# A spectrum scratch laid out by slice, loaded with repeated source rows and stored in halves

## The chip, the cores and the metric

The kernel runs on one core of a Trainium2 chip. The metric is the device time of one execution in microseconds (us). The core has five engines that run their own instruction streams and meet at semaphores: TensorE (PE in the profile, with its weight loads as PEld), VectorE (DVE), ScalarE (ACT), GpSimd (POOL) and SyncE (SP). Here SP only issues transfers; POOL issues some too. Sixteen DMA engines move the data of all transfers.

## The reference

Four layers run one after the other on a sequence of 2048 tokens with 512 channels: a long convolution, an attention over a few neighbours, and both again with the same weights.

```python
x = A_u
x = x + _A_ref(_layernorm(x, axis=-1), ...)   # convolution
x = x + _B_ref(_layernorm(x, axis=-1), ...)   # local attention
x = x + _A_ref(_layernorm(x, axis=-1), ...)
x = x + _B_ref(_layernorm(x, axis=-1), ...)
```

Only the convolution matters here. It builds one filter per channel and multiplies in the frequency domain:

```python
P = jnp.exp(logdA[:, :, None] * l[None, None, :])
K = jnp.einsum("dn,dnl,dn->dl", Cc, P, dB).real
Kf = rfft(pad(K));  Uf = rfft(pad(u))
y = irfft(Uf * Kf)[:, :L] + u * Dskip
```

`Kf`, the spectrum of the filters, depends on the weights alone. Both convolutions use the same one.

## The kernel before, in words

**Making the spectrum (0 to about 126 us).** `kgen` builds tables of powers on VectorE, TensorE and ScalarE for one quarter of 128 channels after the other (`c` from 0 to 3). For each quarter TensorE multiplies the tables (`psk`), ScalarE copies the result (`KT`), and a round trip through a scratch in HBM brings it into another order (`rows_scratch`, L587 and L590). TensorE then turns it into frequencies in four steps (`spectrum`, `i` from 0 to 3, L601 and L606). ScalarE or VectorE writes the result into a tile `ks` of 128 channels x 2 x 512 (L614 to L630). There are four buffers for `ks`. The function `store` (L608) sends each tile to the HBM scratch `kt_scratch` with two transfers. That makes 16 tiles and 32 transfers, all issued by SP.

**Using it (about 119 to 152 us, and again 275 to 306 us).** The convolution runs over 16 slices of 32 channels (`cg`). For each slice TensorE transposes the signal (`pt`), VectorE copies it (`zt`), TensorE does the second stage of the Fourier transform (`xp`), ScalarE copies it (`xc`), VectorE multiplies it with the spectrum (`pab`, L275, the step `p`), TensorE transforms back (`vp`, L291) and ScalarE copies (`VT`, L295). The spectrum of a slice is a tile `Kt` of 128 partitions x 2048 elements, in which each row of 2048 elements stands twice, in an even partition and the odd one after it. `load_k` (L226) loads it from `kt_scratch` with two transfers, one into the even partitions and one into the odd. There are five buffers for `Kt` in the first convolution and six in the second. A load is issued when the product of the slice that had the buffer is done.

**What sets the order.** The order on the compute engines is written out by hand in two strings of step names (`KGEN` and `CONV2`). Transfers stand in the queue of the engine that issues them, in the order that the scheduler puts them. Slices 0 and 1 of the first convolution are issued by POOL, the others by SP. For the first four slices `FIRST_LOADS` names an instruction after which the load may be issued; for slices 2 and 3 that is a store. SP's transfers take eight semaphores in turn, and each transfer waits until the one eight places before it has landed.

Of the kernel before, what the change touches and what calls it, by code (L numbers as in the profile page):

```python
# [15 lines left out]
BF = mybir.dt.bfloat16  # L16
# [4 lines left out]
D = 512  # L21
# [8 lines left out]
GE = 4  # L30
# [4 lines left out]
DCH = 128  # L35
# [72 lines left out]
def make_small_consts(nc, const):  # L108
    fc = _fft_consts()
    C = {}  # L110
    C["F1_h"] = nc.inline_tensor(_bf(fc["F1"]), name="c_F1")
    C["F1T_h"] = nc.inline_tensor(_bf(fc["F1T"]), name="c_F1T")
    C["G_h"] = nc.inline_tensor(_bf(_kernel_dft()), name="c_G")
    bones_np = np.zeros((128, 8), dtype=np.float32)
    for f in range(128):
        bones_np[f, f // 16] = 1.0
    m, b, l, p = (x.ravel() for x in np.meshgrid(np.arange(2), np.arange(2), np.arange(16), np.arange(2), indexing="ij"))
    order = np.zeros((128, 128), dtype=np.float32)
    order[p * 64 + b * 32 + m * 16 + l, np.arange(128)] = 1.0
    small = [("order", _bf(order), BF), ("ident", _bf(np.eye(128)), BF), ("nident", _bf(-np.eye(128)), BF), ("nident4", _bf(-np.eye(128) * DH ** 0.5), BF),  # L120
             ("bones", _bf(bones_np), BF), ("C2", _bf(fc["C2"]), BF), ("IC", _bf(fc["IC"]), BF)]
    for name, arr, dt in small:
        h = nc.inline_tensor(arr, name="c_" + name)
        t = const.tile(list(arr.shape), dt, name="sb_" + name)
        C[name], C[name + "_h"] = t, h
    C["halves_h"] = nc.inline_tensor(_bf(_half_matrices()), name="c_halves")
    C["zero_h"] = nc.inline_tensor(_bf(np.zeros((1, 14 * 256))), name="c_zero")
    C["half_pi"] = const.tile([128, 1], F32, name="half_pi")
    nc.gpsimd.memset(C["half_pi"][:], np.pi / 2)
    C["zero"] = const.tile([128, 1], BF, name="zero_col")  # L130
    nc.gpsimd.memset(C["zero"][:], 0.0)
    C["den_bias"] = const.tile([128, 1], F32, name="den_bias")
    nc.gpsimd.memset(C["den_bias"][:], np.log(DEN_SCALE))
    C["eps"] = const.tile([128, 1], F32, name="eps")
    nc.gpsimd.memset(C["eps"][:], EPS)
    return C


def load_x(nc, const, x2d):
    xv = x2d.rearrange("(p j) d -> p j d", j=NJ)  # L140
    Xg = []
    for g in range(NG):
        t = const.tile([128, 4, D], BF, name=f"X{g}")
        nc.sync.dma_start(t[:], xv[:, g * 4:(g + 1) * 4, :])
        Xg.append(t)
    return Xg
# [24 lines left out]
def first_norm_tiles(small):  # L171
    return {n: small.tile([128, NJ] + e, F32, name="n1_" + n, bufs=1)
            for n, e in (("stats", [6]), ("mv", [2]), ("m2", []), ("den", []), ("rstd", []), ("nb", []))}
# [14 lines left out]
def first_norm_rstd(nc, st, eps, h):  # L188
    c = slice(h * NJ // 2, (h + 1) * NJ // 2)
    nc.scalar.activation(st["den"][:, c], st["m2"][:, c], ACT.Ln, scale=1.0 / D, bias=eps[:])  # L190
    nc.scalar.activation(st["rstd"][:, c], st["den"][:, c], ACT.Exp, scale=-0.5)
# [15 lines left out]
def z_view(Z):  # L207
    return Z[:].rearrange("k (c g) (r j e) -> k r j c g e", c=16, r=2, j=NJ)


def a_steps(nc, tc, C, Ng, kt_dram, load_w, layer, Z, es, es_y, psS=None):
# [4 lines left out]
    a = SimpleNamespace(es_y=es_y)  # L216
# [3 lines left out]
    kts, pts, zts, xps, xcs, pabs, vps = {}, {}, {}, {}, {}, {}, {}  # L220
# [4 lines left out]

    def load_k(cg, eng=nc.sync):  # L226
        kts[cg] = fwork.tile([128, 8, 2, 128], BF, name="Kt", tag="Kt", bufs=KT_BUFS[layer])
        rows = kt_dram.ap()[:, cg * 32:(cg + 1) * 32].rearrange("k (e g) a l -> k e (g a l)", e=GE)
        for h in range(2):
            eng.dma_start(kts[cg][h::2].rearrange("q g a l -> q (g a l)"), rows)  # L230

    def load_f1t():
        nc.sync.dma_start(F1T[:], C["F1T_h"].ap())
# [150 lines left out]
def kgen(nc, tc, C, prm, kt_dram, Zf, norm_row, norm_rstd, norm_apply, norm_apply_row, norm_tiles, load_rest, es_a, es_y, open_conv):  # L384
    everything = KGEN.split()
    with ExitStack() as es:
# [220 lines left out]

        def store(c, i, ks):  # L608
            for k in range(2):
                dst = kt_dram.ap()[k * 8 + i * 2:k * 8 + i * 2 + 2, c * DCH:(c + 1) * DCH]  # L610
                C["stored", c, i] = nc.sync.dma_start(dst.rearrange("k d r l -> d k (r l)"), ks[:, k, :].rearrange("d (k x) -> d k x", k=2))

        def spectrum_odd(c, i):
            ks = tiles["ks", c, i] = keep.tile([128, 2, 512], BF, name="ks", tag="ks", bufs=4)  # L614
# [72 lines left out]
        for c in range(4):  # L687
# [16 lines left out]
            for full in [n for n in everything if n.endswith(f":{c}") and n[0] in "Uv"]:  # L704
# [4 lines left out]
                else:  # L709
                    m = int(key[1:])  # L710
# [42 lines left out]
        for g in range(16):  # L753
# [7 lines left out]
            stored = [f"{'o' if g // 4 * 4 + i in WHOLE else 'e'}{g // 4}{i}" for i in range(4)]  # L761
# [852 lines left out]
@with_exitstack  # L1614
def kernel(
    ctx: ExitStack,
    tc: tile.TileContext,
    A_u: bass.AP,
    A_A_re: bass.AP,
    A_A_im: bass.AP,  # L1620
    A_B_re: bass.AP,
    A_B_im: bass.AP,
    A_C_re: bass.AP,
    A_C_im: bass.AP,
    A_log_dt: bass.AP,
    A_Dskip: bass.AP,
    B_x: bass.AP,
    B_wqkv: bass.AP,
    B_wo: bass.AP,
    out: bass.AP,  # L1630
):
    nc = tc.nc
    const = ctx.enter_context(tc.tile_pool(name="const", bufs=1))
    C = make_small_consts(nc, const)
    kt_dram = nc.dram_tensor("kt_scratch", (16, D, 2, 128), BF)
    C["rows_dram"] = nc.dram_tensor("rows_scratch", (4, 2, 2, 4, NV, 160), BF)
    prm = dict(A_re=A_A_re, A_im=A_A_im, B_re=A_B_re, B_im=A_B_im, C_re=A_C_re, C_im=A_C_im, log_dt=A_log_dt)
    C["out"] = out[0].rearrange("(p j) d -> p j d", j=NJ)
    Xg = []
    Ng = C["Ng"] = []  # L1640
    late = ctx.enter_context(tc.tile_pool(name="late", bufs=1, side="right"))
    C["small"] = ctx.enter_context(tc.tile_pool(name="small", bufs=2, side="right"))
    C["F1"] = late.tile([128, NJ, 2, 128], BF, name="F1sb")
    C["klast"] = late.tile([1, D], BF, name="klast")
    C["signs"] = late.tile([128, 2], BF, name="signs")
    for i in range(2):
        nc.gpsimd.memset(C["signs"][:, i:i + 1], 1.0 - 2 * i)
    C["last_tok"] = late.tile([128, 128], BF, name="last_tok")
    nc.gpsimd.memset(C["last_tok"][:], 0.0)
    nc.gpsimd.memset(C["last_tok"][0:1, 127:128], 1.0)  # L1650
    C["Drow"] = late.tile([128, D], BF, name="Drow")
    nc.gpsimd.memset(C["Drow"][:], 0.0)
    C["first_row"] = late.tile([128, 2 * NV], BF, name="first_row")
    nc.gpsimd.memset(C["first_row"][:], 0.0)
    nc.gpsimd.memset(C["first_row"][0:1, 2 * NV - 2:2 * NV], 1.0)
    n1 = {}

    def load_rest():
        for name in ("ident", "nident", "nident4", "bones", "C2", "IC"):
            nc.gpsimd.dma_start(C[name][:], C[name + "_h"].ap())  # L1660
        nc.gpsimd.dma_start(C["Drow"][0:1, :], A_Dskip.rearrange("(o d) -> o d", o=1))
        Xg.extend(load_x(nc, late, A_u[0]))
        nc.sync.dma_start(C["F1"][:], C["F1_h"].ap())
        n1["st"] = first_norm_tiles(C["small"])

    def norm_row(j, on_act):
        first_norm_row(nc, C["small"], n1["st"], Xg, j, on_act)

    def norm_rstd(h):
        first_norm_rstd(nc, n1["st"], C["eps"], h)  # L1670

    def norm_apply(h):
        first_norm_apply(nc, n1["st"], Xg, Ng, h)

    def norm_apply_row(j, on_act):
        first_norm_apply_row(nc, n1["st"], Xg, Ng, j, on_act)

    def norm_tiles():
        npool = ctx.enter_context(tc.tile_pool(name="normed", bufs=1, side="right", reuse_waits="tile"))
        Ng.extend(npool.tile([128, 4, D], BF, name=f"N{g}") for g in range(NG))  # L1680

    es_z = ExitStack()
    Z = es_z.enter_context(tc.tile_pool(name="a_z", bufs=1, reuse_waits="tile")).tile([128, NGR, 128], BF, name="Z")
    C["z_view"] = z_view(Z)
    es_y = ExitStack()
    Wt = {}

    def open_conv(psS):
        const2 = ctx.enter_context(tc.tile_pool(name="const2", bufs=1, side="right", reuse_waits="tile"))
        weights, load_w = load_b_weights(nc, const2, C, B_wqkv, B_wo)  # L1690
        Wt.update(weights)
        return a_steps(nc, tc, C, Ng, kt_dram, load_w, 0, Z, es_z, es_y, psS)

    a = kgen(nc, tc, C, prm, kt_dram, Z[:].rearrange("k a b -> k (a b)"), norm_row, norm_rstd, norm_apply, norm_apply_row, norm_tiles, load_rest, es_z, es_y, open_conv)
    es_z.close()
    for layer in range(2):
        y_rows, es_y = a_layer(nc, tc, C, Xg, Ng, kt_dram, layer, Z, es_z, a if layer == 0 else None)
        Z, es_z = b_layer(nc, tc, C, Xg, Ng, Wt, layer == 1, y_rows, es_y)
# [30 lines left out]
```

## Time and profile before

The median of three runs is 423.59 us (423.0 to 424.81). The profile is of one more execution.

| | before |
|---|---|
| median of the runs | 423.59 us |
| span of the profiled execution | 421.2 us |
| busy: PE, PEld, DVE, ACT, POOL | 90%, 61%, 94%, 79%, 6% |
| granted TensorE clock | 0.998 |
| DMA bytes, packets | 44.09 MB, 25822 |
| stores of the spectrum | 32 of 128 KB, issued 72.2 to 125.2 us |
| loads of the spectrum | 64 of 256 KB (60 from SP, 4 from POOL) |

The span runs from the first to the last instruction that the profiler recorded. The profile gives no time around it, so the difference of 2.4 us between span and median is taken as what lies outside the span and between executions. All times in views count from the start of the span. The DMA share is the mean busy share of the 16 DMA engines, so four full engines alone would show as 0.25. Times of packets can overlap a little, which is why a share can be a few per cent over 1.

### The profile page before, as it was taken

To read this page: it belongs to the slowest core of one execution; us is meant where nothing else is said; L and a number is where in the kernel's file an instruction comes from. 1 tells how busy PE (TensorE), PEld (TensorE's weight loads), DVE (VectorE), ACT (ScalarE), POOL (GpSimd) and SP (SyncE) were. 2 spreads that over 40 slices of the span, in tenths; PEclk is the share of its full clock that TensorE was granted. 3 is DMA by queue.
4 is the path that set the end of the run, shared out by engine and by line. 5 is a ranking of instruction groups with operands and counts; after the bars stand their busy time and mean duration, and the time that the engine had idled before them with its cause. 6 is when DMAs were issued, how large, how long until landed. Compare 5 with 4: busy or idle time off the path is not lost.

```text
span 421.2 us, 12212 instructions
## 1 busy us (share of the span) xinstructions
PE 377.2 (90%) x5088; PEld 259.0 (61%) x5131; DVE 396.4 (94%) x725; ACT 333.1 (79%) x601; POOL 26.0 (6%) x68
## 2 busy tenths in 40 slices
PE   1167998999989999999999999889999999998996
PEld 1033685676458755587866675278855686775663
DVE  6999999999889979899999999999989999999994
ACT  6999999998979979766665699989989576555452
POOL 5000011011210000002020000000000001200000
PEclk9999999999999999999999999999999999999999
DMA  7910001253899960005480029239500008160022
GB/s 219 424 53 0 3 14 50 76 163 101 256 246 273 259 208 4 2 2 95 83 174 6 2 70 232 103 103 262 139 0 4 2 2 174 37 142 4 2 102 101
DMA packets 25822, 44.09 MB, mean 105 GB/s; under 512 B 7317, under 2 KB 17238, under 8 KB 25126
## 3 DMA queue, kind: packets, MB, share of 16 engines
q1 hardware_dynamic: 22630, 37.30, 31.8%
q0 software_dynamic: 1888, 4.56, 5.0%
q10 hardware_dynamic: 1248, 1.44, 1.0%
q8 instruction: 40, 0.66, 0.7%
q14 instruction: 16, 0.13, 0.1%
HBM read 29.04 MB, written 6.95 MB: 85 GB/s over the span
## 4 chain that ended last, share of the span: by engine, by line
PE 48%; DVE 21%; DMA 8%; ACT 7%; issue 3%; SPq 1%; DVEq 0%; ACTq 0%
PE ps_qk L1207 8%; DVE prodpv L1403 6%; PE ps_o L1443 5%; PE ps_v L1294 5%; DMA V<-V 4%; PE po L1413 4%; DVE prodqk L1257 3%; PE psg L601 3%; PE vp L291 3%; PE Lp L1279 3%; DMA Kt<-kt_scratch 3%; DVE Z L504 2%; PE psk L568 2%; DVE pab L275 2%; ACT Z L1496 2%
## 5 line engine op out<-in xcount | busy, mean ns | idle before, releaser
L1403 DVE TENSOR_TENSOR prodpv<-V,Lsb 128x2048 bf16<-128x2048 bf16 x64 | 75.3, 1219 | 0.6 <-PE ps_max L1342 0.5
L1207 PE MATMUL ps_qk<-xnT,wqk 128*128 128x512 bf16 x256 | 60.0, 379 | 0.0
L1255 DVE TENSOR_TENSOR prodqk<-qT,N 128x1024 bf16<-128x1024 bf16 (+3 forms) x88 | 42.7, 541 | 2.0 <-ACT N L1210 1.8
L1257 DVE TENSOR_TENSOR prodqk<-qT,N 128x1024 bf16<-128x1024 bf16 (+3 forms) x56 | 39.9, 764 | 0.4 <-ACT N L1210 0.3
L275 DVE TENSOR_TENSOR pab<-xc,Kt 128x2048 bf16<-128x2048 bf16 (+1 forms) x34 | 38.8, 1154 | 1.2 <-DMA Kt<-kt_scratch 1.0
L1207 PEld LDWEIGHTS <-wqk 128*128 128x128 bf16 x256 | 23.5, 98 | 23.3
L1413 PEld LDWEIGHTS <-prodpv 128*128 128x128 bf16 x1024 | 33.6, 98 | 6.5 <-DVE prodpv L1403 2.1
L1413 PE MATMUL po<-halves,prodpv 128*128 128x64 bf16 x1024 | 36.5, 193 | 0.8 <-DVE prodpv L1403 0.6
L269 ACT CAST xc<-xp 128x1024 bf16<-128x1024 f32 (+1 forms) x34 | 34.6, 1033 | 2.2 <-PE xp L263 1.2
L291 PE MATMUL vp<-sb_IC,pab 128*128 128x128 bf16 x512 | 33.7, 219 | 1.6 <-DVE pab L275 0.7
L291 PEld LDWEIGHTS <-pab 128*128 128x128 bf16 x512 | 30.3, 98 | 7.4 <-DVE pab L275 4.0
L295 ACT CAST VT<-vp 128x1024 bf16<-128x1024 f32 (+1 forms) x31 | 32.6, 1067 | 1.1 <-PE vp L291 1.1
L1279 PEld LDWEIGHTS <-prodqk 128*128 128x128 bf16 x1024 | 30.1, 96 | 5.0 <-DVE prodqk L1257 1.4
L1443 PE MATMUL ps_o<-wo_t,oT 128*128 128x512 bf16 x124 | 32.3, 379 | 0.4
L1279 PE MATMUL Lp<-sb_bones,prodqk 128*128 128x8 bf16 x1024 | 30.9, 166 | 0.3
L1294 PE MATMUL ps_v<-wv,xnT 128*128 128x256 bf16 x256 | 30.6, 272 | 0.0
L528 PE MATMUL psadd<-Z,sb_ident 128*128 128x512 bf16 (+3 forms) x72 | 18.2, 334 | 13.1 <-DVE Z L504 7.7
L1160 DVE BATCH_NORM_STATS2 ln_stats<-X 128x6 f32<-128x512 bf16 x39 | 25.0, 679 | 2.7 <-ACT X L1549 2.7
L1424 ACT CAST oT<-po 128x512 bf16<-128x512 f32 x32 | 17.8, 589 | 12.0 <-PE po L1413 12.0
L1210 ACT CAST N<-ps_qk 128x512 bf16<-128x512 f32 x32 | 18.5, 585 | 10.7 <-PE ps_qk L1207 10.7
L1294 PEld LDWEIGHTS <-xnT 128*128 128x128 bf16 x256 | 24.2, 97 | 3.2
L1301 ACT CAST V<-ps_v 128x512 bf16<-128x512 f32 x32 | 17.5, 592 | 9.9 <-PE ps_v L1294 9.9
(199 smaller groups left out, 833.5 us busy)
## 6 DMA issues: line engine op xcount, KB each, us to landing
Kt<-kt_scratch SPq DMA_DIRECT2D x60, 256.0 KB, 5.7
kt_scratch<-ks SPq DMA_DIRECT2D x32, 128.0 KB, 3.2
G<-c_G SPq DMA_DIRECT2D x2, 1536.0 KB
V<-V SPq DMA_DIRECT2D x8, 288.0 KB, 7.8
X<-in_A_u_dram SPq DMA_DIRECT2D x4, 512.0 KB, 5.9
F1Tsb<-c_F1T SPq DMA_DIRECT2D x2, 1024.0 KB
V<-V SPq DMA_DIRECT2D x4, 512.0 KB
V<-V POOLq DMA_DIRECT2D x4, 384.0 KB, 7.7
```

The source lines that it names most:

```text
L269: nc.scalar.copy(xcs[cg][:, gs].rearrange("q g o l -> q (g o l)"), xps[cg][:].rearrange("q h n -> q (h n)")[:, gs.start * 128:gs.stop * 128])
L275: nc.vector.tensor_tensor(pabs[cg][:, gs], xcs[cg][:, gs].to_broadcast([128, gs.stop - gs.start, 2, 128]), kts[cg][:, gs], ALU.mult)
L291: a.last_pe = nc.tensor.matmul(vp[:, g, :], pabs[cg][:, gs.start + g, ab, :], C["IC"][:, ab, :], start=(ab == 0), stop=(ab == 1))
L295: copy(dst[..., parts(cg)[part]], vps.pop((cg, part))[:].rearrange("k g (q e) -> k q e g", e=GE))
L1207: nc.tensor.matmul(t.ps[:], wqk[:, ct, f0:f0 + 128], x_group(g)[:, :, ct], start=(ct == 0), stop=(ct == 3))
L1255: nc.vector.tensor_tensor(b.pr[:, u:u + 2 * n, 1 - halves_of[0], :], q, cols(kT[i][:, starts[0]:starts[0] + n * 128]), ALU.mult)
L1257: nc.vector.tensor_tensor(b.pr[:, u:u + 2 * n].rearrange("f u a q -> f a u q")[:, ::-1], q.unsqueeze(1).to_broadcast([128, 2, 2 * n, 64]), ...
L1279: nc.tensor.matmul(t.Lp[:, w, u % 2, u // 2, :], b.pr[:, u].rearrange("f a q -> f (a q)"), bones[:], start=False, stop=(t.parts == W // 2 ...
L1294: nc.tensor.matmul(t.ps[:, jj, :], tokens(ct, jp * 2 + jj, c), wv[:, ct, fp * 256:(fp + 1) * 256], start=(jj + ct == 0), stop=(jj == 1 and ...
L1403: nc.vector.tensor_tensor(t.p2[:, c:c + k, 0:nj, :].rearrange("p c j (d h) -> p c j d h", d=DH), m.V2[i // 2][:, c0 + c:c0 + c + k, r0:r0 ...
L1413: nc.tensor.matmul(po[jj // k][:, jj % k, c, :], t.p2[:, c - c0, jj, :], fold, start=(first and c == c0 and jj % k == 0), stop=(last and c ...
L1443: nc.tensor.matmul(t["ps"][:], m.oT[:, ft, j * 128:(j + 1) * 128], wo_t[:, ft, :], start=(start and ft == lo), stop=(ft == 3 or kept and f ...
```

## The change

The scratch `kt_scratch` was ordered by frequency block first and channel second. It is now ordered by slice of 32 channels first, then frequency block, then channel within the slice. A slice lies in one block of 256 KB.

A load is now one transfer. Its source names each row of 4 KB twice (a step of 0 with a count of 2), and its destination is all 128 partitions in order.

A tile `ks` covers four slices and, for each `k`, two frequency blocks. The new order of the scratch splits each old store in two: one transfer for each `k` and each of the two blocks `m`. The destination of one is 4 slices x 32 channels x 256 elements.

```diff
     def load_k(cg, eng=nc.sync):
         kts[cg] = fwork.tile([128, 8, 2, 128], BF, name="Kt", tag="Kt", bufs=KT_BUFS[layer])
-        rows = kt_dram.ap()[:, cg * 32:(cg + 1) * 32].rearrange("k (e g) a l -> k e (g a l)", e=GE)
-        for h in range(2):
-            eng.dma_start(kts[cg][h::2].rearrange("q g a l -> q (g a l)"), rows)
+        rows = kt_dram.ap()[cg].rearrange("k (e g) a l -> (k e) (g a l)", e=GE)
+        eng.dma_start(kts[cg][:].rearrange("q g a l -> q (g a l)"), rows.unsqueeze(1).to_broadcast([16 * GE, 2, 8 * 256]))
...
         def store(c, i, ks):
             for k in range(2):
-                dst = kt_dram.ap()[k * 8 + i * 2:k * 8 + i * 2 + 2, c * DCH:(c + 1) * DCH]
-                C["stored", c, i] = nc.sync.dma_start(dst.rearrange("k d r l -> d k (r l)"), ks[:, k, :].rearrange("d (k x) -> d k x", k=2))
+                for m in range(2):
+                    dst = kt_dram.ap()[c * 4:(c + 1) * 4, k * 8 + i * 2 + m]
+                    C["stored", c, i] = nc.sync.dma_start(dst.rearrange("s d r l -> s d (r l)"), ks[:, k, m * 256:(m + 1) * 256])
...
-    kt_dram = nc.dram_tensor("kt_scratch", (16, D, 2, 128), BF)
+    kt_dram = nc.dram_tensor("kt_scratch", (16, 16, 32, 2, 128), BF)
```

The order of instructions on PE, DVE and ACT is the same in both programs. On SP it moves in one place: before, loads of slice 2 and later stood between the stores of the last quarter; now the stores of all but the last two tiles stand ahead of the load of slice 2. Then come the loads of slices 2, 3 and 4, a tile's four stores, the load of slice 5, the last tile's four stores, and the loads of slices 6 to 15.

## The prediction

> **What bounds the kernel now.** I read the page first, then the chain of waits from 98 to 152 us, then, for that stretch, SP's and VectorE's timelines, the busy table by windows, and the DMA view in narrow windows. From the page: the span, the 40 slices of DMA share, and the transfers that the diff touches.
>
> ```profile
> span 421.2 us, 12212 instructions
> DMA  7910001253899960005480029239500008160022
> DMA packets 25822, 44.09 MB, mean 105 GB/s; under 512 B 7317, under 2 KB 17238, under 8 KB 25126
> ...
> Kt<-kt_scratch SPq DMA_DIRECT2D x60, 256.0 KB, 5.7
> kt_scratch<-ks SPq DMA_DIRECT2D x32, 128.0 KB, 3.2
> ...
> rows<-rows_scratch POOLq DMA_DIRECT2D x4, 160.0 KB, 2.8
> ```
>
> The 16 DMA engines are idle in many slices but full in slices 12 to 14 (116 to 147 us). That is where the spectrum has just been stored and the first convolution loads it back. The windows give the share there, and the chain shows both transfers on the path:
>
> ```profile
> core 0: us, PE busy (x) PEld busy (x) DVE busy (x) ACT busy (x) POOL busy (x), PEclk, DMA share, GB/s
> 103.00:126.00 23.00, 20.81 (x135) 11.35 (x136) 19.87 (x33) 19.29 (x28) 4.53 (x14) 1.00 0.84 237
> 126.00:151.00 25.00, 23.22 (x327) 19.58 (x332) 23.85 (x28) 25.00 (x29) 0.00 (x0) 1.00 1.01 273
> ```
>
> ```profile
> 107.00 2.42 DMA kt_scratch<-ks
> 109.42 1.29 DVE ks L630 x2
> ...
> 143.07 6.85 DMA Kt<-kt_scratch
> 150.04 0.70 DVE pab L275
> ```
>
> Two things are to be seen. At 109.42 VectorE writes a `ks` tile only after a store has landed: there are four `ks` buffers, so late stores stop the spectrum. At 150.04 the last product waits for the last load. VectorE's idle time is still small, one wait in this stretch, and there is none in the second convolution:
>
> ```profile
> 150.04 1.29 DVE L275 TENSOR_TENSOR pab<-xc,Kt 128x1024 bf16<-128x1024 bf16 x2 [1.04 <-DMA Kt<-kt_scratch]
> ```
>
> ```profile
> L230 SPq DMA_DIRECT2D Kt<-kt_scratch x32: 514/592/975, 248.7 to 294.8; - x32
> its engine sat idle before it (us, times) until:
> who waited for it (us, times):
>   PEld L291: 1.0, 3
> ```
>
> So this stretch is bound by VectorE and ScalarE with the DMA engines full just beneath them: 8 MB of loads and the last stores share them with almost no room.
>
> **The change, part by part.** *Prices of rows.* Three narrow DMA windows: 76.9 to 79.5 us (two stores alone), 136 to 142 (loads of `Kt` alone), 403 to 408 (one store of 4 KB output rows).
>
> ```profile
> DMA packets 544, 0.26 MB, mean 101 GB/s; under 512 B 32, under 2 KB 544, under 8 KB 544
> q1 hardware_dynamic: 544, 0.26, 34.2%
> ```
>
> ```profile
> DMA packets 477, 1.57 MB, mean 262 GB/s; under 512 B 94, under 2 KB 94, under 8 KB 477
> q1 hardware_dynamic: 477, 1.57, 103.2%
> ```
>
> ```profile
> q1 hardware_dynamic: 144, 0.52, 26.7%
> ```
>
> The share times 16 engines times the width gives engine time. Stores: 0.342 x 16 x 2.6 = 14.2 us for 512 rows of 512 B and 32 small packets, about 27 ns a row. `Kt` rows of 4 KB: 1.032 x 16 x 6 = 99 us over 383 rows, 256 ns a row with the small ones taken off. Output rows of 4 KB: 0.267 x 16 x 5 = 21.4 us over 128, 166 ns.
>
> *The stores.* 32 transfers of 128 KB become 64 of 64 KB, the same rows of 512 B. Before, the outermost count of the destination was 128 channels. Now it is 4 slices, each followed by 32 channels; the source keeps 128 rows. What matters is how many engines share such a transfer. The two stores above brought 32 small packets, 16 each. Four one-row transfers (163 to 168 us) brought four in all, beside four of data, so small packets count engines:
>
> ```profile
> DMA packets 8, 0.02 MB, mean 4 GB/s; under 512 B 4, under 2 KB 4, under 8 KB 8
> V<-c_zero SPq DMA_DIRECT2D x2, 3.0 KB
> V<-c_zero SPq DMA_DIRECT2D x2, 7.0 KB
> ```
>
> So 128 rows went to 16 engines and one row to one. No row shows an outermost 4 against 128. The bounds are 16 engines (a tile `ks`, 512 rows in all, costs each 32 rows, 0.87 us) and 4 engines (128 rows, 3.47 us). I take 4: in both observed kinds the engine count divides the outermost count, and no count that divides 4 exceeds 4. I also take the same four each time, as nothing in the program names others; dealt round all 16 they would cost as little as in rival 1.
>
> [...]
>
> *Where that lands.* The `ks` view, with issue times and landings of the stores; SP's order around the last nine tiles (here ten transfers are five tiles); and what VectorE then needs:
>
> ```profile
> L611 SPq DMA_DIRECT2D kt_scratch<-ks x32: 359/372/565, 72.2 to 125.2; - x32
> ...
> DMA to landing us min/median/max: 1.8/3.2/4.1
> ```
>
> ```profile
> 103.90 9.37 SPq L611 DMA_DIRECT2D kt_scratch<-ks  x10
> 113.37 0.57 SPq L230 DMA_DIRECT2D Kt<-kt_scratch  x1
> 114.49 0.96 SPq L611 DMA_DIRECT2D kt_scratch<-ks  x2
> ...
> 124.55 1.05 SPq L611 DMA_DIRECT2D kt_scratch<-ks  x2
> ```
>
> ```profile
> 126.12 1.22 DVE L275 TENSOR_TENSOR pab<-xc,Kt 128x2048 bf16<-128x2048 bf16 x1
> 133.65 1.22 DVE L275 TENSOR_TENSOR pab<-xc,Kt 128x2048 bf16<-128x2048 bf16 x1
> ```
>
> ```profile
> 107.00 2.03 POOL L230 DMA_DIRECT2D Kt<-kt_scratch  x4 [0.31 <-DVE ks L630]
> ```
>
> In the new program's SP order seven tiles of `ks` (28 stores) stand from here before the load of slice 2; then slices 2, 3, 4, a tile, slice 5, the last tile, slices 6 to 15. SP holds at most eight transfers on the way (eight semaphores in turn), so a store that waits also stops the loads behind it. Five tiles took SP 9.37 us, so one becomes ready every 2 us; four engines need 3.47 each, so those four run without a gap. I follow one of them, with a slice of `Kt` costing 8 rows: 1.33 us at 166 ns or 2.05 at 256.
>
> First byte about 105.2 (the store at 103.90 plus 1.3: the quickest store lands 1.8 after its issue, and 0.43 of that are its 16 rows per engine). Seven tiles 24.3, the load of `rows` 0.6 (10 KB per engine), slices 0 and 1 from POOL 2.7 or 4.1: 132.8 or 134.2. Slice 2: 134.1 or 136.2, landed 0.7 later (an estimate from the same 1.8); its product was at 126.12, so 8.7 or 10.8 late. Slices 3 and 4, a tile, slice 5, the last tile, slice 6: 4 x 1.33 + 6.9 = 12.3, or 4 x 2.05 + 6.9 = 15.1, so 146.4 or 151.3, landed 147.1 or 152.0. The product of slice 6 was at 133.65: 13.4 or 18.4 late. Nine more slices take 12.0 or 18.5. The last lands at 159.1 or 170.5 against a product at 150.04: 9.1 or 20.4. So the delay at the end is the larger one in each case: **+13.4 with fast rows, +20.4 with slow ones**. The four `ks` buffers make part of this appear earlier, as VectorE and TensorE waiting near 114 to 118; it is the same delay, not a second one.
>
> *The loads.* 64 transfers become 32, the bytes are the same, and each source slice is now one block of 256 KB instead of 16 pieces of 16 KB at steps of 256 KB. The outermost counts are 64 and 128, so 16 engines stay. SP saves 32 issues of 0.59 us, off the path: it mostly waits. Bounds for a row: 256 ns as now, 166 as the output rows, which lie in long runs. I take 166, since the new source is like those. Alone this is worth at most the 1.04 us wait at 150.04. In the second convolution no VectorE wait is on a load, so 0 there; if that cover were gone, each load that came late would hold VectorE for its lateness.
>
> [...]
>
> *Sum.* 421.2 + 13.4 = 434.6 us of span. The median of the runs shown is 423.59, 2.4 above the span; I carry that along: **437 us**.
>
> **Rivals.**
> 1. *Stores stay on 16 engines* (not slower). Then a tile costs 0.87 us as before, 32 more store issues of 0.37 us stand against 32 fewer load issues of 0.59, and faster loads take away the 1.04 us: 422.5 us. For it: the source side has 128 rows that could be dealt out. Against: the one-row transfers. It decides if the new small packets number 16 per store.
> 2. *Four engines and slow load rows*: +20.4, 444 us. For it: all `Kt` rows in this trace took 256 ns when many were on the way. Against: output rows.
> 3. *Four engines, but quicker store rows.* At the byte rate of the 166 ns rows, 512 B take 21 ns; nine tiles save 0.8 us each, 7.4 in all: +6.0, 430 us. Against: 27 ns was measured with the engines otherwise free.
>
> **Chances.** Four engines with fast or middling rows (my forecast) 0.60; rival 2 0.18; rival 3 0.07; rival 1 0.11; anything else 0.04. Range 428 to 448: from below rival 3 to rival 2 plus 3 ns per store row (9 x 128 x 3 ns = 3.5 us). It leaves out rival 1 and a little more. A change of 0.5%, 2.1 us, is about what can be told here; rival 1 lies within it for the most part. Faster 0.05, same 0.09, slower 0.86.
>
> **What would show it.** Packets: 64 stores with 4 small packets instead of 32 with 16, and 32 loads with 16 instead of 64, give 768 fewer: 25,054 in all and 6,549 under 512 B. Rival 1 keeps 25,822 and 7,317. Stores should land 7 to 10 us after issue in the 105 to 125 us stretch instead of 3.2; VectorE should wait for stores before `ks` and for loads before `pab`; the share of DMA in 110 to 130 us should fall though it is the bottleneck. The second convolution should keep its length. I am wrong if stores land as fast as before, or if the delay sits outside 105 to 150 us.

## The result and the profile after

The changed kernel takes 435.06 us (median; 432.66 to 436.61), the kernel before 423.58 us beside it on the same chip. The ratio is 1.0265 with a 95% interval of 1.0226 to 1.0303: 2.3 to 3.0% slower. The forecast was 437 us. The profiled execution spans 430.9 us against 421.2, 9.7 us more.

The page of the changed kernel, its DMA row in 40 slices, its packets and its two transfers:

```profile
DMA  7900001253527981000843008118400007160022
DMA packets 25054, 44.09 MB, mean 102 GB/s; under 512 B 6549, under 2 KB 16470, under 8 KB 24358
...
Kt<-kt_scratch SPq DMA_DIRECT2D x30, 512.0 KB
kt_scratch<-ks SPq DMA_DIRECT2D x64, 64.0 KB
```

The packets are exactly the forecast ones: 25,054, and 6,549 under 512 B. So each new store has four small packets, not 16. In slices 11 to 13 of the DMA row (108 to 140 us) stands 5 2 7 where it was 8 9 9 (105 to 137 us).

The windows by busy time (us, engines with their counts, granted clock, DMA share, GB/s) for the stretch that the prediction spoke of, its five worst microseconds, and five microseconds in which the loads run alone:

```profile
103.00:126.00 23.00, 18.30 (x90) 8.57 (x88) 15.01 (x27) 15.01 (x24) 3.74 (x13) 0.93 0.42 128
120.00:125.00 5.00, 3.72 (x22) 1.94 (x22) 2.76 (x5) 1.07 (x2) 1.03 (x7) 0.66 0.29 86
145.00:150.00 5.00, 4.51 (x67) 3.74 (x67) 4.79 (x6) 4.42 (x5) 0.00 (x0) 1.00 1.02 389
```

From 103 to 126 us the DMA share has halved (0.84 before, 0.42 now) and VectorE is busy 15.0 us instead of 19.9. Once the stores are through, the loads fill all sixteen engines and move 389 GB/s, where 126 to 151 us had 273 before: their rows have got quicker. An idle core beside idle DMA engines looks like no bottleneck at all; the 0.29 of 120 to 125 us is four engines of sixteen with a little over, and those four have no gap, as the even row of the DMA view for 120 to 128 us shows:

```profile
DMA  2222222222222222222222222222222222222222
...
DMA packets 1393, 0.69 MB, mean 86 GB/s; under 512 B 43, under 2 KB 1393, under 8 KB 1393
...
q1 hardware_dynamic: 1393, 0.69, 28.8%
```

SP's timeline (start, length, what it issues, how many) and, from VectorE's, three waits and the last products (the wait before the instruction in brackets; the last line has none):

```profile
104.30 23.72 SPq L611 DMA_DIRECT2D kt_scratch<-ks  x28
128.12 1.92 SPq L229 DMA_DIRECT2D Kt<-kt_scratch  x3
130.13 3.08 SPq L611 DMA_DIRECT2D kt_scratch<-ks  x4
133.33 2.23 SPq L229 DMA_DIRECT2D Kt<-kt_scratch  x1
135.66 2.52 SPq L611 DMA_DIRECT2D kt_scratch<-ks  x4
138.29 15.54 SPq L229 DMA_DIRECT2D Kt<-kt_scratch  x10
```

```profile
119.75 1.29 DVE L630 TENSOR_TENSOR ks<-psg,odd 128x512 bf16<-128x512 f32 x2 [3.08 <-DMA kt_scratch<-ks]
...
133.13 1.23 DVE L274 TENSOR_TENSOR pab<-xc,Kt 128x2048 bf16<-128x2048 bf16 x1 [1.97 <-DMA Kt<-kt_scratch]
...
144.21 1.22 DVE L274 TENSOR_TENSOR pab<-xc,Kt 128x2048 bf16<-128x2048 bf16 x1 [2.45 <-DMA Kt<-kt_scratch]
...
157.29 3.66 DVE L274 TENSOR_TENSOR pab<-xc,Kt 128x2048 bf16<-128x2048 bf16 x4
```

The product of slice 2 was at 126.12 and is at 133.13: 7.0 late. That of slice 6 was at 133.65 and is at 144.21: 10.6 late. The last product ended at 150.04 + 1.29 = 151.33 and ends at 157.29 + 3.66 = 160.95: 9.6 late, as much as the whole span grew. The second convolution only starts later. Its products, before and after (count, shortest, median, longest, first and last start):

```profile
L275 DVE TENSOR_TENSOR pab<-xc,Kt x17: 686/1219/1226, 277.6 to 304.3; 128x2048 bf16<-128x2048 bf16 x15, 128x1024 bf16<-128x1024 bf16 x2
```

```profile
L274 DVE TENSOR_TENSOR pab<-xc,Kt x17: 685/1215/1224, 287.7 to 314.0; 128x2048 bf16<-128x2048 bf16 x15, 128x1024 bf16<-128x1024 bf16 x2
```

26.7 us from first to last product before, 26.3 after.

### The profile page after: what moved, and what is told of

It is laid out like the page before. It is cut to its first block, busy times and chain, and to the rows that moved or that the text cites. A ratio compares the mean times of both kernels' runs of the same rounds, so it can differ in the third digit from the quotient of the medians.

```text
span 430.9 us, 12259 instructions
## 1 busy us (share of the span) xinstructions
PE 381.3 (88%) x5131; PEld 258.7 (60%) x5131; DVE 396.8 (92%) x725; ACT 333.8 (77%) x601; POOL 25.2 (6%) x66
## 2 busy tenths in 40 slices
DMA packets 25054, 44.09 MB, mean 102 GB/s; under 512 B 6549, under 2 KB 16470, under 8 KB 24358
## 4 chain that ended last, share of the span: by engine, by line
PE 47%; DVE 22%; DMA 8%; ACT 7%; issue 3%; SPq 2%; DVEq 0%; ACTq 0%
PE ps_qk L1207 8%; DVE prodpv L1403 8%; PE ps_o L1443 5%; DVE prodqk L1257 4%; DMA Kt<-kt_scratch 4%; PE po L1413 4%; PE vp L290 4%; PE psg L600 3%; PE ps_v L1294 3%; PE Lp L1279 3%; DVE Z L503 2%; PE psk L567 2%; ACT Z L1496 2%; DMA V<-V 2%; DMA kt_scratch<-ks 2%
## 5 line engine op out<-in xcount | busy, mean ns | idle before, releaser
L268 ACT CAST xc<-xp 128x1024 bf16<-128x1024 f32 (+1 forms) x34 | 33.5, 1000 | 6.3 <-DVE pab L274 4.5
L290 PEld LDWEIGHTS <-pab 128*128 128x128 bf16 x512 | 30.0, 98 | 12.5 <-DVE pab L274 10.6
L1443 PE MATMUL ps_o<-wo_t,oT 128*128 128x512 bf16 x128 | 33.2, 379 | 0.0
L294 ACT CAST VT<-vp 128x1024 bf16<-128x1024 f32 (+1 forms) x31 | 31.5, 1042 | 0.3
L527 PE MATMUL psadd<-Z,sb_ident 128*128 128x384 bf16 (+3 forms) x75 | 19.0, 340 | 12.9 <-DVE Z L503 7.5
L1210 ACT CAST N<-ps_qk 128x512 bf16<-128x512 f32 x32 | 18.5, 585 | 11.2 <-PE ps_qk L1207 11.1
```

Source lines behind the costliest of these rows:

```text
L268: nc.scalar.copy(xcs[cg][:, gs].rearrange("q g o l -> q (g o l)"), xps[cg][:].rearrange("q h n -> q (h n)")[:, gs.start * 128:gs.stop * 128])
L290: a.last_pe = nc.tensor.matmul(vp[:, g, :], pabs[cg][:, gs.start + g, ab, :], C["IC"][:, ab, :], start=(ab == 0), stop=(ab == 1))
L294: copy(dst[..., parts(cg)[part]], vps.pop((cg, part))[:].rearrange("k g (q e) -> k q e g", e=GE))
L1443: nc.tensor.matmul(t["ps"][:], m.oT[:, ft, j * 128:(j + 1) * 128], wo_t[:, ft, :], start=(start and ft == lo), stop=(ft == 3 or kept and f ...
```

## The experiments

The theory, A: the delay comes from the stores' outermost count of 4, which puts each of them on four engines. The rivals: B, the layout by slice or the single large load is slow by itself; D, it is the 64 stores instead of 32, whatever engines they use; F, it is only the place of the loads in SP's queue. All times are medians; the kernel before took 423.1 to 423.3 us beside them, and 424.81 (one run) beside the slice layout on two engines.

**Sixteen engines again, first try.** The slice layout and its loads stay. Each store covers the 32 channels of one slice, so 32 stands outermost, but it takes 128 stores. Once all on SP, once every second one on POOL:

```diff
-                for m in range(2):
-                    dst = kt_dram.ap()[c * 4:(c + 1) * 4, k * 8 + i * 2 + m]
-                    ... nc.sync.dma_start(dst.rearrange("s d r l -> s d (r l)"), ks[:, k, m * 256:(m + 1) * 256])
+                for q in range(4):
+                    dst = kt_dram.ap()[c * 4 + q, k * 8 + i * 2:k * 8 + i * 2 + 2].rearrange("m d r l -> d m (r l)")
+                    ... (nc.gpsimd if q % 2 else nc.sync).dma_start(dst, ks[q * 32:(q + 1) * 32, k].rearrange("d (m x) -> d m x", m=2))
```

> The changed kernel with its slice layout and its loads, but each store cut along the channels, so that 32 channels stand outermost: 128 stores of 32 KB, two slices of each tile issued by SP and two by POOL. Theory A (the delay comes from stores confined to four engines): a tile costs each engine 32 rows again, VectorE waits for a store before `ks` or for a load before `pab` for 1.5 us in all at most, and the time is 421 to 426 us (the 128 POOL and SP issues may cost 2 us); 26,846 packets, 8,341 under 512 B, if each store has 16 small ones. Rival B (the layout by slice is slow to write, or single transfers of 512 KB are slow to land, however many engines): it stays at 432 to 437 us.

> The same as the run before it, with all 128 stores issued by SP. Theory A with 0.37 us an issue: eight issues are 3.0 us a tile against one tile every 2 us; seven tiles take 7 us longer than the tiles come, so the loads start some 6 us late and the time is 426 to 431 us, with the DMA engines' share low and SP issuing without a gap. Rival B: 432 to 437 us, or more by the same issues. Rival C (issues overlap with nothing to lose): 421 to 424.

Two queues: 430.68 us. One queue: 444.16 us. Both miss, and neither decides between A and B by its time. Both have 8,341 small packets, 16 a store. With one queue all packets are the expected 26,846, with two only 23,774; that stores issued by POOL come in fewer packets had not been foreseen. With two queues SP gets through its 28 stores in 14.44 us instead of 23.72, but slice 0's load now stands behind POOL's own 28 stores. Its POOL and VectorE timelines:

```profile
107.90 14.87 POOL L611 DMA_DIRECT2D kt_scratch<-ks  x28
...
123.23 0.62 POOL L229 DMA_DIRECT2D Kt<-kt_scratch  x1
```

```profile
129.18 1.23 DVE L274 TENSOR_TENSOR pab<-xc,Kt 128x2048 bf16<-128x2048 bf16 x1 [6.47 <-DMA Kt<-kt_scratch]
```

That one wait of 6.47 us is nearly the whole loss: an edit that cured one queue had filled another. With one queue SP's issues are the limit: 56 stores follow each other for 28.36 us, 0.51 us each.

```profile
108.68 28.36 SPq L611 DMA_DIRECT2D kt_scratch<-ks  x56
```

**Fewer engines alone.** The kernel before, old layout and old loads, with each store cut in two along the channels. Only the numbers of the cut change what divides them:

```diff
+                dst = kt_dram.ap()[k * 8 + i * 2:k * 8 + i * 2 + 2, c * DCH:(c + 1) * DCH].rearrange("k d r l -> d k (r l)")
+                src = ks[:, k, :].rearrange("d (k x) -> d k x", k=2)
+                for p in (slice(0, 116), slice(116, 128)):     # 112 + 16; 104 + 24; 122 + 6
+                    C["stored", c, i] = nc.sync.dma_start(dst[p], src[p])
```

> The kernel before (old layout, old loads, rows of 4 KB at 255 ns), with each store cut into 116 and 12 channels: 116 = 4 x 29, so by theory A the large part runs on four engines, 116 + 4 of a tile's 512 rows on each. At 21 ns a row a tile is 2.5 us on those four; with the slow load rows the last product is 10 to 16 us late, so 433 to 440 us. Rival B (layout or load form): no change beyond the issues, 423 to 426 us. Packets if theory A holds: 64 stores, 32 with 4 and 32 with 12 small ones, as many as the 32 with 16 before: 25,822 and 7,317 unchanged.

> The control of the run before it: the same 64 stores in the old layout, cut into 112 and 16 channels, both of which 16 divides. Theory A: 16 engines for both, 423 to 426 us. Rival D (64 stores instead of 32, with twice the fixed cost and twice SP's issues, make the delay): as late as with 116 and 12, 433 us or more. Packets by theory A: 64 x 16 small ones, 512 more than before: 26,334 and 7,829 under 512 B.

> The kernel before with each store cut into 104 and 24 channels: 104 = 8 x 13 runs on eight engines, 24 on twelve, so the busiest engines have 60 of a tile's 512 rows: 1.4 to 1.6 us at 24 to 27 ns a row, less than the 2 us in which a tile becomes ready. Theory A (a limit that bites only when a tile's rows take longer than a tile): as late as with 112 and 16 channels (428.6 us), 427 to 431. If instead the delay grows in step with the rows per engine: 33 rows gave +5.3, 120 gave +13.4, so 60 would give +7.8, 431 us or more.

> The kernel before with each store cut into 122 and 6 channels: 122 = 2 x 61, so by theory A the large part runs on two engines, 248 of a tile's 512 rows on each. A tile then takes 5.2 us at 21 ns a row, or 6.7 us at 27 ns; seven tiles follow each other without SP's issues in the way, so the spacing gives the price of a row. From the run with 116 and 12 (436.7 us) nine tiles take 9 x 128 more rows: 24 us later at 21 ns, 31 us at 27 ns, so 461 or 468 us. Rival (engines do not share by the outermost count): 425 to 437 us.

| cut | engines of the larger part, by small packets | time, us | ratio, 95% interval | over the kernel before |
|---|---|---|---|---|
| 112 + 16 | 16 | 428.61 | 1.0119, 1.0092 to 1.0146 | +5.3 |
| 104 + 24 | 13 | 428.22 | 1.0097, 1.0065 to 1.0129 | +4.9 |
| 116 + 12 | 4 | 436.70 | 1.0312, 1.0287 to 1.0337 | +13.4 |
| 122 + 6 | 2 | 478.32 (one run) | | +55 |

The small packets tell the engines. All other transfers have 6,805 (7,317 before, less 16 for each of 32 stores), so the two stores that an old one was cut into have 32 together with 112 + 16 (7,829 under 512 B in all), 25 with 104 + 24 (7,605), 16 with 116 + 12 (7,317) and 8 with 122 + 6 (7,061). I read them as 16 + 16, 13 + 12, 4 + 12 and 2 + 6; each count divides its channels. So 104 channels went to thirteen engines, not to the eight of the expectation, and the busiest engines had 40 of a tile's 512 rows, not 60. A holds, with the old layout and the old loads, so B isn't needed. Sixteen and thirteen engines cost the same, four are 8 us worse, two far worse. A tile becomes ready every 2 us. At 23.7 ns a row (measured below) the busiest engines' 40 rows of it take 0.9 us with thirteen engines, and 120 rows take 2.8 us with four. Whether the delay sets in only where a tile's rows take longer than a tile, or grows in step with them, the run with 104 + 24 can't tell: with 40 rows the expectation's own line from 33 rows to 120 gives about +6 us, too near +5.3 to be told from it, and no run stands between 40 and 120 rows. But D holds too, for a part: 64 stores on 16 engines cost 5.3 us, which the expectation had put at 0 to 3. In that run the last ten loads leave SP at 131.51 us instead of 125.77, and VectorE waits 5.0 us in all for loads, whose rows took 251 ns in the kernel before. With 64 stores SP's order has also become that of the changed kernel, 28 stores ahead of the load of slice 2, so the 5.3 us are the price of the count and of this order together; no run separates the two. Rows of its SP timeline:

```profile
104.17 15.85 SPq L613 DMA_DIRECT2D kt_scratch<-ks  x28
...
131.51 17.03 SPq L230 DMA_DIRECT2D Kt<-kt_scratch  x20
```

The two-engine run came later than either price of a row allowed, because I had counted the last nine tiles alone: there the earlier quarters' stores are already too slow, and the stretch of 28 stores starts at 120.44 us instead of 104.10 with four engines.

**The price of a row.** The same run has a stretch, 145 to 155 us, in which stores alone run and do not stop. To see whether the layout or the number of engines sets the price, the changed kernel was also run with each of its stores cut into two slices and two:

```diff
-                    dst = kt_dram.ap()[c * 4:(c + 1) * 4, k * 8 + i * 2 + m]
+                    for p in range(2):
+                        dst = kt_dram.ap()[c * 4 + p * 2:c * 4 + p * 2 + 2, k * 8 + i * 2 + m]
...
```

> The changed kernel with each store cut in two, two slices each: 128 stores of 32 KB with an outermost count of 2, so two engines, 256 of a tile's rows on each. In the stretch in which the two have no gap, count the rows. If a 512 B row is cheap because an engine writes 32 of them into one run of 16 KB (slice layout): 23.7 ns, as in the changed kernel, 6.1 us a tile. If the price depends on how many engines share: 26.8 ns, as in the run with 122 and 6 channels, 6.9 us a tile. Time 465 to 485 us either way.

The DMA view from 145 to 155 us, first of the old layout on two engines, then of the slice layout on two:

```profile
DMA packets 896, 0.45 MB, mean 45 GB/s; under 512 B 26, under 2 KB 896, under 8 KB 896
...
q1 hardware_dynamic: 896, 0.45, 14.8%
```

```profile
DMA packets 870, 0.43 MB, mean 43 GB/s; under 512 B 26, under 2 KB 870, under 8 KB 870
...
q1 hardware_dynamic: 870, 0.43, 14.4%
```

Slice layout: 844 rows on two engines, 422 each in 10 us, 23.7 ns a row. Old layout: of 870 rows each of the two has 248 in 512, so 421 in 10 us, 23.7 ns. The changed kernel on four engines, 120 to 128 us (above): 1,350 rows, 337.5 each in 8 us, 23.7 ns. So neither the layout nor the number of engines, two or four, matters to the price, and the 26.8 ns in my expectation was no price: it came from 130 to 160 us of the two-engine run, where POOL's slices took part of the engines. The run took 479.16 us (one run).

**Sixteen engines, same 64 stores.** The clean form of the first try. The 16 frequency rows of the scratch are put in the order tile, half, row, so that the four rows of one tile in one slice are evenly spaced and one store can take them all, with 32 channels outermost. The same order goes into the two small transform matrices, so the product still meets the right rows:

```diff
-    k2 = np.arange(16)
+    k2 = np.arange(16).reshape(2, 4, 2).transpose(1, 0, 2).reshape(16)
...
+            for q in range(4):
+                dst = kt_dram.ap()[c * 4 + q, i * 4:i * 4 + 4].rearrange("n d r l -> d n (r l)")
+                C["stored", c, i] = nc.sync.dma_start(dst, ks[q * 32:(q + 1) * 32].rearrange("d k (m x) -> d (k m) x", m=2))
```

> The changed kernel (scratch by slice, one load of 512 KB a slice) with the same count and size of stores, 64 of 64 KB, but 32 channels outermost in place of 4 slices: the frequency rows of the scratch and of the two small transform matrices are put in the order tile, half, row, so that one slice's four rows of a tile are evenly spaced. Theory A (four engines): a store lands 2 to 3 us after its issue, VectorE's waits for stores and loads fall under 1.5 us, seven tiles take SP 15 to 17 us instead of 23.7, and the time is 421 to 426 us. Rival D (64 issues of 0.45 us, or the layout): seven tiles still take over 20 us and the time is 430 to 437 us. 25,822 packets, 7,317 under 512 B.

425.24 us, ratio 1.0049 (1.0032 to 1.0065). Count and size of all transfers, and the place of the stores ahead of the loads, are those of the changed kernel; what differs is that a store takes four rows of each of 32 channels in place of one row of 4 x 32, so that 32 stands outermost. 9.8 of the changed kernel's 11.5 us are gone. Its transfers, SP's seven tiles and the waits for transfers that are left on VectorE in this stretch:

```profile
Kt<-kt_scratch SPq DMA_DIRECT2D x30, 512.0 KB, 4.8
kt_scratch<-ks SPq DMA_DIRECT2D x64, 64.0 KB, 2.1
```

```profile
106.12 16.37 SPq L610 DMA_DIRECT2D kt_scratch<-ks  x28
```

```profile
116.42 1.29 DVE L629 TENSOR_TENSOR ks<-psg,odd 128x512 bf16<-128x512 f32 x2 [2.08 <-DMA kt_scratch<-ks]
...
153.20 1.29 DVE L274 TENSOR_TENSOR pab<-xc,Kt 128x1024 bf16<-128x1024 bf16 x2 [0.21 <-DMA Kt<-kt_scratch]
```

Stores land 2.1 us after their issue. The 2 us that remain are mainly one wait for a store before `ks`; with the last load the waits come to 2.3 us, more than the 1.5 expected. B and the larger part of D fall.

**The loads on another queue.** The changed kernel, with every slice of the first convolution issued by POOL instead of only slices 0 and 1:

```diff
-            load_k(cg, nc.gpsimd if layer == 0 and FIRST_LOADS[cg][0] == "rows_end" else nc.sync)
+            load_k(cg, nc.gpsimd if layer == 0 else nc.sync)
...
-                  ..., k=load_k, ...
+                  ..., k=lambda cg: load_k(cg, nc.gpsimd), ...
```

> The changed kernel with its four-engine stores, but all 16 slices of the first convolution loaded from POOL's queue instead of two; slices 2 to 7 belong to quarters stored long before, so nothing but their place in the queue holds them back. Theory F (the delay is the queue: slices stand behind 28 stores on the same four engines in SP's queue): slices 2 to 4 land by 120 us, VectorE's waits before `pab` fall from 5.3 us to under 2, the 3.1 us wait for a store before `ks` stays, and the time is 425 to 430 us. Rival G (the four engines have no time for both, whatever the queue): their rows come at the same rate, the waits stay or move, 432 to 437 us.

439.85 us, ratio 1.0380 (1.0346 to 1.0414), worse than the change and above the range of both theories. The loads did get past the stores, and the stores paid. VectorE's timeline:

```profile
125.03 1.29 DVE L630 TENSOR_TENSOR ks<-psg,odd 128x512 bf16<-128x512 f32 x2 [8.50 <-DMA kt_scratch<-ks]
...
132.28 1.22 DVE L274 TENSOR_TENSOR pab<-xc,Kt 128x2048 bf16<-128x2048 bf16 x1
...
160.78 1.23 DVE L274 TENSOR_TENSOR pab<-xc,Kt 128x2048 bf16<-128x2048 bf16 x1 [5.46 <-DMA Kt<-kt_scratch]
```

The wait before `ks` grows from 3.08 to 8.50 us. From the first product (132.28 instead of 122.05, 10.2 late) eleven products run without a wait for a load, where the changed kernel waited three times. So the 10 us have only moved: the four engines have this much to do, whichever queue goes first. F falls, and G holds in its mechanism. The second wait, 5.46 us, comes from the same four engines: slices 12 to 15 belong to the last quarter, and the chain of waits has that quarter's last store on the way from 139.91 us for 12.20 us, so POOL's last four loads leave only at 152.66 us. SP, free of loads, had sent the attention's weights from 141.63 us on, and they fill the engines just then (share 1.11 from 153 to 156 us); what part of the wait is theirs is not separated.

**Why the load rows got quick.** Three runs: the changed kernel with its loads in the two old halves; the kernel before with a wider step between the pieces of a slice; and the kernel before with the scratch ordered by quarter, so that the pieces lie 64 KiB apart:

```diff
-        eng.dma_start(kts[cg][:].rearrange("q g a l -> q (g a l)"), rows.unsqueeze(1).to_broadcast([16 * GE, 2, 8 * 256]))
+        for h in range(2):
+            eng.dma_start(kts[cg][h::2].rearrange("q g a l -> q (g a l)"), rows)
```

```diff
-    kt_dram = nc.dram_tensor("kt_scratch", (16, D, 2, 128), BF)
+    kt_dram = nc.dram_tensor("kt_scratch", (16, D + 8, 2, 128), BF)
```

```diff
...
-    kt_dram = nc.dram_tensor("kt_scratch", (16, D, 2, 128), BF)
+    kt_dram = nc.dram_tensor("kt_scratch", (4, 16, DCH, 2, 128), BF)
```

> The changed kernel with its layout and its four-engine stores, but each slice loaded by the two old transfers, one for each half of the partition pairs. Theory A1 (load rows are quick because a slice is one block of 256 KB): rows of 4 KB stay at 160 to 190 ns, and the time is that of the changed kernel with 32 more issues, 433 to 438 us. Rival A2 (they are quick because source rows are named twice in one transfer): rows at about 255 ns, and the end as with the old loads and four engines (436.7 us) or later, 437 to 443 us.

> The kernel before with 8 channels of room after each of the 16 frequency rows of the scratch: the step from piece to piece of a slice is 260 KiB instead of 256 KiB; stores, loads, counts and sizes are as before. Theory (the power-of-two step makes the load rows slow): 4 KB rows at 160 to 190 ns, the share of DMA in 126 to 151 us falls from 1.01 to about 0.7, the 1.04 us wait at the end goes: 422.0 to 423.3 us beside 423.3. Rival (only one block of 256 KB is quick): 255 ns, share 1.0, no change.

> The kernel before with its stores and its loads as they are, and the scratch ordered by quarter: a slice's 16 pieces of 16 KB stand 64 KiB apart instead of 256 KiB, inside a block of 1 MB. If the quick rows come with pieces that lie close: 4 KB rows at 180 to 200 ns, share of DMA in 126 to 151 us at 0.8 or less, the last 1.04 us wait gone, 422.0 to 423.0 us against 423.1 to 423.6. If only one whole block of 256 KB is quick: 230 to 255 ns, share about 1.0, no change.

The rows are first compared in the second convolution, where the loads meet only one other transfer. The DMA view's row for SP's queue, 35 us each: the changed kernel from 265 us, its form with half loads from 265, then the wider step from 255 and the quarters from 255:

```profile
q1 hardware_dynamic: 1399, 5.61, 44.2%
```

```profile
q1 hardware_dynamic: 1581, 5.75, 47.5%
```

```profile
q1 hardware_dynamic: 1543, 5.65, 57.6%
```

```profile
q1 hardware_dynamic: 1580, 5.75, 51.8%
```

Share times 16 times 35 us over the megabytes gives, per 4 KB: 181 ns, 189, 234 and 207; the kernel before has 58.1% and 5.45 MB from 255 us, 245 ns. These are sums of packet records, which serve to compare like with like. The price that an engine needs is again a count of rows where all sixteen are full, and the changed kernel has such a stretch in the first convolution. The DMA view from 143 to 149 us:

```profile
DMA packets 621, 2.28 MB, mean 380 GB/s; under 512 B 67, under 2 KB 67, under 8 KB 620
...
q1 hardware_dynamic: 620, 2.27, 96.9%
```

That is 553 rows of 4 KB on 16 engines in 6 us, at most 174 ns a row; 145 to 150 us, with no gap, has 471 rows, 170 ns. The kernel before has 383 rows from 136 to 142 us (the window of the prediction), 251 ns. Half loads have 455 rows from 146 to 151 us, 176 ns. So the one block per slice makes the rows quick (A1), and naming them twice does not (A2): the same two half loads are quick with it. The other two forms give no clear answer. From 136 to 142 us the wider step has 424 rows (226 ns) and the quarters 390 (246 ns); in the second convolution, where the kernel before has 260 ns (255 to 262 us), the wider step has 259 (255 to 262 us) and the quarters 215 (255 to 261 us). Each is quicker in one place and hardly in the other, and neither comes near 170. Both miss the quick rows that they were built to show: from 126 to 151 us the share of SP's queue stays at 98.1% and 99.3%, and the last wait shrinks from 1.04 us to 0.40 and 0.61.

The times are 433.98 us with half loads (ratio 1.0267, like the change), 422.74 with the wider step (0.9993, 0.9984 to 1.0002) and 423.40 with the quarters (0.9997, 0.9980 to 1.0014). No form of quicker rows by itself can be told from the kernel before, and none of the runs beats it.

## Why the prediction was right, and where its sizes were off

The step that carried the forecast holds: the stores with 4 outermost ran on four engines, and on the same four. Their four small packets each show the four. That they were the same four each time follows from the even DMA row at 0.29 while stores queue (7.57 us to landing), and from the price: 1,350 rows on four engines give the same 23.7 ns as the runs on two; the trace does not name a packet's engine. The run with the same stores and 32 outermost gives 9.8 us back.

The place holds too: SP's 28 stores ahead of slice 2, waits before `ks` and `pab`, a low DMA share in the stretch that it limits, the second convolution unchanged. Stores were to land 7 to 10 us after issue; the chain of waits has the last one before `ks` at 7.57 us. That "it is the same delay, not a second one", said of the four `ks` buffers, agrees with the run with POOL's loads, where the waits moved from the loads to the stores. One reading of the lines was too strong: the wait for a store at 109.42 us in the kernel before cost VectorE nothing, since its cast of 108.81 us ran until 109.50; that store landed just in time.

The forecast was +13.4 us of span, measured are +9.7. The term that was mis-sized is the row of 512 B: 27 ns forecast, 23.7 measured when nothing else runs. Over nine tiles that is 9 x 128 x 3.3 ns = 3.8 us. The step that failed is the reading of share times engines times width as time that an engine needs. The records of neighbouring packets overlap: on two engines without a gap the share is 14.4% of 16, 2.3 engines. Counting rows per engine in a stretch without a gap would have given the price; the two stores of 76.9 to 79.5 us were too short for it. Rival 3, with 21 ns and a chance of 0.07, was the other bound; the truth lies between them, nearly midway, and what I held against that rival, that "27 ns was measured with the engines otherwise free", did not exclude it. For two prices about equally far from the truth, chances of 0.60 and 0.07 were too far apart.

Two smaller terms cancel. With 23.7 ns the working gives slice 2 landed at 134.8 - 7 x 128 x 3.3 ns = 131.8 us, and its product came at 133.13, 1.3 later; why is not settled (from 108 to 112 us the four engines were not full). From there to slice 6 the working gives 12.3 - 0.8 = 11.5 us, measured 11.1. And 13.4 late at slice 6 was carried to the end as it stood, although the kernel before waits 1.04 us for a load just there: that wait is gone now, so the end is 1.0 less late than slice 6, 9.6 against 10.6.

The load rows: 166 ns was taken and 170 came, counted from 145 to 150 us, so the choice of quick rows, taken from the output rows, was right. That the step of 256 KiB had made them slow is not shown: 4 KiB of padding on it moved a row from 251 to 226 ns in one convolution and from 260 to 259 in the other, while one block moved it to 170.

Rival 1's price was too low. With 16 engines and 64 stores it gave 422.5 us, and the run gives 425.24: twice the stores, with the order on SP that came with them, were not free here. The median of the changed kernel stands 11.5 us above the kernel before, its profiled span 9.7. Each of its four runs has 1.8 to 1.9 us of time outside its span, so the 2.4 us that the prediction carried along held some spread between executions too, and 437 beside 435.06 us looks closer than +13.4 beside +9.7 is. The profiled run is the quickest of the four. The other three have spans of 433.0, 433.4 and 434.7 us, and their mean granted clock falls in the same order, from 0.996 in the profiled run to 0.994, 0.992 and 0.984; whether that is the cause is not shown.

## What to carry to other kernels

Before reordering a transfer, look at the outermost count on both sides. Here the stores with 4 slices outermost on one side ran on four engines and those with 2 on two, and while DMA was the bottleneck its share stood at 0.29 and 0.14; so read that share against the number of engines that take part, which the small packets counted here. Price a row by counting rows per engine in a stretch without a gap, not by adding up packet times (23.7 ns against 27 here). When stores and loads share a queue, count what stands ahead of the first load that is needed; moving loads to another queue did not help here (439.85 us against 435.06), since both needed the same engines.

## What had not been expected of the hardware

Issuing a store takes SP a median of 0.54 us with 4 outermost, 0.44 with 32 and 0.37 with 128 (the `ks` views: 536, 435 and 372 ns), though the bytes are 64, 64 and 128 KB. The stores differ in more than this count, so what sets the time is not shown. Single issues take over 2 us (2,364 ns, the longest of the changed kernel), and SP issues nothing else meanwhile.

The granted TensorE clock falls to 0.66 in 120 to 125 us, after TensorE had waited 3.06 us for `ks`:

```profile
121.09 2.72 PE L605 MATMUL psg<-G,rows 128*128 128x512 bf16 x6 [3.06 <-DVE ks L630]
```

Six matmuls take 2.72 us there, where five of the same took 1.24 us at 115.93 us. Over the whole run the clock is 0.996 here and 0.946 and 0.950 in the two runs on two engines. So the matmuls right after the wait for the late transfer were slower here; that the wait itself lowered the clock is my reading, and no run shows it alone.
